# Softmax denominators of a memory attention: nine bf16 blocks on TensorE, or a GpSimd sum in three bf16 terms

## The chip, the cores and the metric

The kernel runs on one core of a Trainium2 chip. The metric is the device time of one launch in microseconds, the median of the runs shown. All times inside the kernel come from one profiled execution on the chip.

## The reference

The program has two parts. The first is an attention through 32 memory slots per head; the second is a channel mix of the RWKV kind on its output. Shapes: q, k, v are (8, 8, 576, 64) for batch, head, position and head width, phi is (8, 8, 576, 32), all in f32.

```
a    = exp(phi - max over positions); a = a / (sum over positions of a + 1e-9)
k_m  = sum over s of a[s, m] k[s, d];   v_m likewise with v
attn = softmax over m of (q k_m^T / 8);  x = attn v_m        (heads joined: 8 x 576 x 512)
x_prev = x shifted by one position
xk = mu_k x + (1 - mu_k) x_prev;   xr likewise with mu_r
out = sigmoid(xr w_r) * (relu(xk w_k)^2 w_v)
```

What the change touches is the sum over positions of exp(phi), one number for each head and slot. The kernel leaves out the maximum, which cancels in the quotient.

## The kernel before

The 576 positions of a batch are laid out as 64 rows of 9, so that one batch of phi fills 128 partitions (2 groups of 64 rows) by 4 heads by 9 positions by 32 slots. `exp_phi` (L225, word `exp`) takes a batch of phi on ScalarE and writes bf16 `em`, 128 x 9 x 4 x 32; there are two `em` tiles, for even and odd batches, and two buffers `ph` for raw phi. `ekv` (L237, word `kv`) multiplies `em` with k and v on TensorE in 72 small matmuls. `esum` (L247, word `z`) does the denominators: nine matmuls, one for each of the nine positions of a row, each with a 128 x 128 block of `em` as weights and a two-column tile of ones as moving data, accumulated in PSUM; VectorE takes the reciprocal `rz`. `norm_k` and `norm_v` (words `nk`, `nv`) scale by it, and the attention goes on: `tk` transposes the keys, `q0`, `q1` (or, for batches 6 and 7, `qx`, a transposing DMA on the SP queue) the queries, `s0`, `s1` are scores, `l0` to `l3` the second softmax's denominators, `r..z` and `w..` its weights, `x0`, `x1` the values, copied out by ScalarE, and `dd`, `k0d`, `k2d`, `r0d`, `r2d` the mix with the previous position on VectorE.

The channel mix runs over tokens: `c0:` to `c8:` are key products with relu on ScalarE (L524) and square on VectorE (L528), `g:` the gates of 128 tokens (L543 to L551), `o:` the value products, their product with the gate (L567) and the stores on the SP queue, from four `o` buffers. All PSUM tiles share eight banks under one name.

Nothing is scheduled automatically. `PLAN` is a list of words written out by hand, and every word emits its instructions in that place, for all engines; each engine then runs its own in that order and waits on the others by semaphores. A number before the colon is the batch; `p:` words are first loads. `load` of batch b issues the four loads of batch b + 2 (phi, k, v, q, in the order of `LOADS`) from GpSimd's queue, which issues in order. A phi load may start once the exp two batches earlier has read its `ph` buffer; the k, v and q loads likewise follow their earlier readers. With `SUMS` empty, no batch has the word `zr`, and `sum_rows` isn't called.

In the attention of the first two batches the mix is folded into the value products (`mk`, `mr`, L288 to L449), and the `idle` matmuls of `busy2` (L195) fill a place where TensorE waits.

Of the kernel before, what the change touches and what calls it, by code (L numbers as in the profile page):

```python
# [15 lines left out]


PLAN = [
    "p:q:0a p:k:0b 0:exp1 0:exp0 0:k0c 0:z 0:qh0 0:k1c 0:hn0 0:ht0 0:s0 p:q:0b 0:hn1 p:v:0a 0:qh1 0:l0 0:ht1 0:l1",
    "0:s1 0:mub p:v:0b 0:l2 p:wr:0-4 p:wk:0-4 0:h1z 0:v0c 0:h0z 0:nr0 0:v1c p:phi:1 0:h2z 0:l3 0:y1 0:y0 p:wk:4-8",  # L20
    "0:h3z 0:nr1 0:busy2 0:y2 0:y3 0:nk0 0:nk1 0:mr0 0:mr1 0:mk0 0:mk1 c0:2a c0:0a g:2 1:exp c0:3a c0:2b c0:5b c0:4b",
    "g:3 1:z c0:6a g:0 p:k:1 1:k 1:nk c0:6b p:q:1 c0:7b c0:0b c0:3b 1:q0 1:q1 0:mu 1:tk c0:5a c0:1a c0:4a p:v:1 1:s1",
    "1:s0 c0:1b 1:v 1:l2 1:l0 c0:7a 1:nr0 p:wv:0-2 p:wv:2-4 1:nk0 1:h0z 1:l3 1:l1 1:h2z 1:nr1 1:h1z 1:h3z g:1 o:3a",
    "1:y2 1:y3 o:2a 1:nk1 1:y0 1:y1 o:2b o:3b 1:mk1 o:0a 1:mk0 1:mr0 c1:0 c1:2 c1:4 1:mr1 g:4 c1:6 c1:3 0:load 2:exp",
    "g:5 2:q0 2:q1 o:1a 7:load 2:z 2:kv 2:nk 2:nv o:0b 2:tk c1:1 2:s1 2:s0 c1:7 c1:5 2:l0 2:l2 2:l1 2:l3 2:r0z 2:r1z",
    "2:w0 2:w1 o:1b o:5 o:4 1:load 3:exp 2:x0 3:q0 g:6 3:z 3:q1 3:kv 2:x1 3:nk g:7 3:nv 3:tk 2:dd 2:k0d g:8 3:s0 3:s1",
    "2:load 2:k2d o:6 4:exp o:7 2:r0d 3:l0 c2:1 c2:5 3:l3 3:l2 4:z 3:l1 c2:0 3:r1z 3:w1 3:r0z 3:w0 c2:4 2:r2d c2:2",
    "c2:3 c2:7 3:x1 4:kv 3:load c2:6 3:x0 4:nk 4:nv g:10 3:dd 3:k0d g:11 3:k2d g:9 5:exp 4:tk 4:q1 4:q0 o:9 o:10 c3:7",
    "c3:0 o:8 5:z 4:s0 5:kv 4:load 3:r0d 4:s1 5:q1 6:exp 5:q0 6:qx 5:nk c3:5 c3:4 4:l1 3:r2d 4:l2 c3:3 5:nv 4:l3 4:l0",
    "5:tk 4:r1z c3:6 g:12 c3:2 6:z 6:kv 6:nv 5:s0 4:r0z 5:load 5:s1 4:w1 4:w0 c3:1 g:13 6:nk o:11 g:14 6:tk 4:x0 o:13",  # L30
    "4:x1 g:15 4:dd o:12 5:l3 4:k0d 5:l0 5:l1 5:r0z o:14 5:l2 4:k2d g:16 7:exp 4:r0d 5:r1z o:15 c4:1 c4:3 7:z 7:kv",
    "6:s1 5:w0 5:w1 6:s0 c4:5 c4:0 5:x0 7:nv 4:r2d 7:nk c4:2 6:l1 c4:4 c4:6 6:l2 c4:7 7:qx 6:l3 5:x1 5:dd g:18 5:k2d",
    "g:19 7:tk 6:l0 g:17 o:18 5:k0d 6:r1z o:16 o:19 7:s1 6:r0z 7:s0 c5:3 c5:1 c5:7 6:w0 g:20 7:l2 c5:2 6:w1 7:l0 7:l1",
    "c5:6 7:l3 5:r2d c5:0 c5:5 c5:4 7:r1z 5:r0d 6:x1 o:17 6:x0 g:21 7:r0z 6:dd 6:k2d o:20 o:21 7:w1 g:22 6:k0d g:23",
    "7:w0 o:23 o:22 6:r2d c6:2 7:x1 c6:5 c6:1 6:r0d 7:x0 c6:4 g:24 7:dd c6:0 6:load c6:7 c6:3 c6:6 g:25 g:26 7:k0d",
    "7:r0d 7:k2d g:27 o:25 o:24 o:26 c8:0 c7:5 c8:6 7:r2d g:28 o:27 g:29 c7:6 c7:0 c7:4 c8:2 g:30 c7:1 c7:2 c7:7 c7:3",
    "g:31 c8:7 c8:4 o:29 c8:3 o:28 o:31 g:32 c8:5 o:30 c8:1 g:33 g:34 o:33 g:35 o:32 o:34 o:35",
]

LOADS = {None: ("phi", "k", "v", "q"), 2: ("phi", "k", "q", "v"), 3: ("phi", "k", "q", "v"), 4: ("phi", "k", "q", "v")}  # L40
PRE = "k:0a id:"
SUMS = ()


NJ = 9
# [4 lines left out]
def kernel(  # L50
# [13 lines left out]
    nc = tc.nc  # L64
# [146 lines left out]
    def attention(b):  # L211
        st = {}

        def ps_tile(shape, dtype, name):
            return psum.tile(shape, dtype, name=name, tag="ps", bufs=8)
# [5 lines left out]
        x0 = b * S % RING  # L221
        kv5, em = kvs[b % 2], ems[b % 2]
# [20 lines left out]
        def esum():  # L243
            st["zps"] = ps_tile([128, 2], F32, "zps")
            parts = [em[:, j].rearrange("p h m -> p (h m)") for j in range(NJ)] if b not in SUMS else st["es"]
            for i, part in enumerate(parts):
# [5 lines left out]
        def sum_rows():  # L252

            left = work.tile([128, HH * M], F32, name="es", tag="es", bufs=1)
            nc.vector.reduce_sum(left, em.rearrange("p j h m -> p (h m) j"), axis=mybir.AxisListType.X)
            terms = work.tile([128, 3, HH * M], BF16, name="et", tag="et", bufs=1)
            for i in range(3):
                nc.vector.tensor_copy(terms[:, i], left)
                if i < 2:
                    nc.vector.tensor_sub(left, left, terms[:, i])  # L260
            st["es"] = [terms[:, i] for i in range(3)]

        def hold():
# [173 lines left out]
        def mixed(w, hf):  # L437

            def go():
# [7 lines left out]
                for i in range(ND):  # L447
# [5 lines left out]
        steps = {"exp": exp_phi, "kv": ekv(slice(0, 2)), "k": ekv(slice(0, 1)), "v": ekv(slice(1, 2)),  # L453
                 "z": esum, "nk": norm_k(), "nv": norm_v, "tk": tr_k(), "load": reload, "mu": load_mu, "mub": load_mu_b, "qx": cross_q,
                 "zr": sum_rows, "hold": hold}
        for i in range(2):
            steps[f"q{i}"] = tr_q(i)
# [163 lines left out]
```

## Time and profile before

| | |
|---|---|
| median of 3 runs | 208.88 us (208.71 to 209.04) |
| profiled execution | 208.39 us, its span 206.6 us |
| mean granted TensorE clock | 0.999 |
| HBM read, written | 38.28 MB, 9.44 MB |
| exp(phi) of a whole batch, L225 | 7 times, 1166 ns |
| phi loads by GpSimd | 7, 576 KB each, median 15.7 us from issue to landing |
| key squares on VectorE, L528 | 104 instructions, 32.7 us |
| mixes on VectorE, L423 and L424 | 48 times 364 ns, 24 times about 759 ns |

In the span's rows PE is the matmul part of TensorE, PEld its weight loads, DVE is VectorE, ACT ScalarE, POOL GpSimd, SP the engine that issues stores. A group's line names engine, operation, what it writes and reads, the count, busy time and mean duration, and the idle time of the engine before it. A matmul's duration is its latency; matmuls follow one another at a shorter pitch. Idle time of an engine that isn't on the chain that ended last costs nothing. The time of the execution is 1.8 us longer than the span.

### The profile page before, as it was taken

The page shows a single profiled execution, that of the slowest core. Times are in us where ns is not written, and L with a number is a line of the kernel's source. Part 1 is how long each engine was busy: PE and PEld are TensorE (multiplying, and loading weights), DVE is VectorE, ACT ScalarE, POOL GpSimd, SP SyncE. Part 2 cuts the span into 40 slices and gives each one's busy share as a digit, 9 for nine tenths or more (in the row PEclk, how much of TensorE's full clock was granted, in tenths as well). Part 3 has the DMA queues.
Part 4 walks back from the last instruction along what each step waited for, and adds up shares of the span by engine and source line. Part 5 has one row for each costly group of instructions (what it writes and reads, how often), then busy time and mean ns, then how long its engine had stood idle before and what let it go on. Part 6 is the DMA issues. An engine that isn't in the chain of part 4 may idle for free.

```text
span 206.6 us, 5609 instructions
## 1 busy us (share of the span) xinstructions
PE 193.9 (94%) x2269; PEld 103.5 (50%) x2269; DVE 135.4 (66%) x364; ACT 159.5 (77%) x314; POOL 29.4 (14%) x45
## 2 busy tenths in 40 slices
PE   0499999999999999999999999999999999999992
PEld 0355676746555545466445764444434444444451
DVE  1129445866478989988749779487978944533232
ACT  3256899978778999978999799989878955882570
POOL 7652422201414102150000000000000000000000
PEclk9999999999999999999999999999999999999999
DMA  6999999999999999999999850502260062004335
GB/s 161 173 204 262 210 208 202 261 230 285 215 273 239 256 279 213 260 231 307 208 157 211 126 87 16 124 17 52 54 154 0 0 152 54 0 0 112 91 71 135
DMA packets 29274, 32.49 MB, mean 157 GB/s; under 512 B 6704, under 2 KB 24384, under 8 KB 29248
## 3 DMA queue, kind: packets, MB, share of 16 engines
q0 software_dynamic: 17392, 20.91, 53.8%
q1 hardware_dynamic: 11088, 10.37, 23.3%
q10 hardware_dynamic: 768, 0.85, 1.3%
q8 instruction: 18, 0.29, 0.6%
q14 instruction: 8, 0.07, 0.1%
HBM read 38.28 MB, written 9.44 MB: 231 GB/s over the span
## 4 chain that ended last, share of the span: by engine, by line
PE 92%; DMA 3%; POOL 1%; DVE 1%; issue 1%; POOLq 0%; DVEq 0%
PE pk L520 31%; PE pv L565 31%; PE pr L543 15%; PE kvps L237 4%; DMA kv<-in_k_dram 3%; PE mxps L288 2%; PE zps L372 2%; PE scps L358 2%; PE qtps L339 2%; PE nops L288 2%; PE zps L247 1%; PE ktps L301 1%; PE mub L200 1%; PE qtps L326 1%; DVE o L567 0%
## 5 line engine op out<-in xcount | busy, mean ns | idle before, releaser
L520 PE MATMUL pk<-xkT,wk 128*128 128x512 bf16 (+4 forms) x352 | 69.0, 341 | 0.0
L565 PE MATMUL pv<-wv,sq 128*128 128x512 bf16 (+1 forms) x328 | 66.2, 353 | 0.0
L528 DVE TENSOR_TENSOR sq<-rl 128x512 bf16<-128x512 bf16 (+5 forms) x104 | 32.7, 341 | 33.3 <-ACT rl L524 32.5
L524 ACT ACTIVATE rl<-pk 128x512 bf16<-128x512 f32 (+3 forms) x80 | 42.9, 560 | 13.4 <-PE pk L520 10.6
L520 PEld LDWEIGHTS <-wk 128*128 128x128 bf16 x352 | 32.7, 98 | 27.8 <-issue 1.6
L565 PEld LDWEIGHTS <-sq 128*128 128x128 bf16 x328 | 31.5, 98 | 29.9 <-issue 0.5
L543 PE MATMUL pr<-wr,xrT 128*128 128x512 bf16 x144 | 35.8, 380 | 0.0
L567 DVE TENSOR_TENSOR o<-sg,pv 128x512 f32<-128x512 f32 (+1 forms) x41 | 24.9, 620 | 15.0 <-PE pv L565 8.7
L548 ACT ACTIVATE sg<-pr 128x512 f32<-128x512 f32 x36 | 21.5, 610 | 8.8 <-PE pr L543 8.8
L543 PEld LDWEIGHTS <-xrT 128*128 128x128 bf16 x144 | 13.5, 98 | 14.8 <-issue 0.2
L550 ACT ACTIVATE sg<-sg 128x1024 f32<-128x1024 f32 x18 | 19.0, 1057 | 0.6
L551 ACT ACTIVATE sg<-sg 128x1024 f32<-128x1024 f32 x18 | 19.0, 1057 | 0.6
L401 ACT CAST x<-nops 128x320 bf16<-128x320 f32 (+1 forms) x48 | 15.7, 419 | 2.4 <-PE nops L288 2.3
L237 PE MATMUL kvps<-kv,em 64*32 64x128 bf16 (+1 forms) x720 | 8.7, 218 | 7.8 <-DMA kv<-in_k_dram 7.8
L423 DVE TENSOR_SCALAR mu_d<-diff,mu 128x576 bf16<-128x576 bf16 x48 | 15.5, 364 | 0.1
L362 ACT ACTIVATE e<-scps 128x320 bf16<-128x320 f32 (+1 forms) x32 | 11.0, 415 | 4.3 <-PE scps L358 4.2
L389 DVE TENSOR_TENSOR atn<-e,lz 128x576 bf16<-128x576 bf16 (+2 forms) x20 | 12.0, 631 | 1.4 <-ACT lz L382 1.3
L377 ACT ACTIVATE lz<-zps 128x320 f32<-128x320 f32 (+1 forms) x32 | 11.7, 413 | 0.8 <-PE zps L372 0.8
L237 PEld LDWEIGHTS <-em 64*32 64x32 bf16 x720 | 7.5, 95 | 8.9 <-ACT em L225 6.1
L225 ACT ACTIVATE em<-ph 128x1152 bf16<-128x1152 f32 (+1 forms) x9 | 9.4, 1056 | 2.3 <-DMA ph<-in_phi_dram 2.3
L382 ACT ACTIVATE lz<-lz 128x576 f32<-128x576 f32 (+2 forms) x20 | 11.1, 587 | 0.1
L413 DVE TENSOR_TENSOR diff<-x 128x1024 bf16<-128x1024 bf16 (+1 forms) x18 | 9.0, 552 | 2.4 <-ACT x L401 2.4
(65 smaller groups left out, 143.7 us busy)
## 6 DMA issues: line engine op xcount, KB each, us to landing
out_dram<-o SPq DMA_DIRECT2D x61, 128.0 KB, 2.4
ph<-in_phi_dram POOLq DMA_DIRECT2D x7, 576.0 KB, 15.7
kv<-in_k_dram POOLq DMA_DIRECT2D x7, 576.0 KB, 15.8
q<-in_q_dram POOLq DMA_DIRECT2D x7, 576.0 KB, 17.9
kv<-in_v_dram POOLq DMA_DIRECT2D x7, 576.0 KB, 19.3
out_dram<-o SPq DMA_DIRECT2D x18, 64.0 KB, 5.5
wk<-in_moe_w_k_dram POOLq DMA_DIRECT2D x2, 512.0 KB, 14.8
wv<-in_moe_w_v_dram POOLq DMA_DIRECT2D x2, 512.0 KB, 20.3
```

The costliest lines, as they stand in the source:

```text
L237: nc.tensor.matmul(kvps[c][g * M:(g + 1) * M], lhsT=em[ROWS[c], j, g, :], rhs=kv5[ROWS[c], parts, g, j, :], start=j == 0, stop=j == NJ - 1 ...
L401: nc.scalar.copy(st["x"][:, i, sl], pss[i])
L423: nc.vector.tensor_scalar_mul(t[:, i], st["d"][:, pr + i, :], mu1[:, o:o + 1])
L520: nc.tensor.matmul(pk[:, p0 - lo:p1 - lo], lhsT=wk_sb[:, di, fi * 128:(fi + 1) * 128], rhs=xk_T[:, di, p0 % RING:p0 % RING + p1 - p0], sta ...
L524: nc.scalar.activation(rl, pk, AF.Relu)
L528: nc.vector.tensor_mul(sq[:, fi, p:p + p1 - p0], rl[:, p0 - lo:p1 - lo], rl[:, p0 - lo:p1 - lo])
L543: nc.tensor.matmul(pr, lhsT=xr_T[:, di, c0:c0 + 128], rhs=wr_sb[:, di, :], start=(di == 0), stop=(di == ND - 1))
L548: nc.scalar.activation(sg[:, t % 2], pr, AF.Exp, scale=-1.0)
L550: nc.scalar.activation(sg, sg, AF.Ln, bias=1.0)
L551: nc.scalar.activation(sg, sg, AF.Exp, scale=-1.0)
L565: nc.tensor.matmul(pv[:, cols], lhsT=sq[:, fi, p:p + 128], rhs=wv_sb[:, fi, cols], start=(fi == 0), stop=(fi == NF - 1))
L567: nc.vector.tensor_mul(o[:, cols], gated[t // 2][:, t % 2, cols], pv[:, cols])
```

## The change

For batches 2 to 7, `SUMS` is filled and the list has a word `zr`. `sum_rows` then has GpSimd add the nine 128 x 128 blocks of `em` into an f32 tile with eight adds, and split the sum into three bf16 terms: convert, subtract, convert, subtract, convert. `esum` takes these three terms as weights in place of the nine blocks, so that it has three matmuls instead of nine. The f32 tile and the terms have one buffer each. The whole list is in a new order; besides the six `zr` words, its words are the same but for `busy2`, which is now `busy3`, with three idle matmuls. Batches 0 and 1 keep nine matmuls. In the new list every `load` from `1:load` to `5:load` stands behind the `zr` of the batch before the one that it loads.

```diff
--- before.py
+++ after.py
@@ -16,30 +16,31 @@
 
 
 PLAN = [
-    "p:q:0a p:k:0b 0:exp1 0:exp0 0:k0c 0:z 0:qh0 0:k1c 0:hn0 0:ht0 0:s0 p:q:0b 0:hn1 p:v:0a 0:qh1 0:l0 0:ht1 0:l1",
-    "0:s1 0:mub p:v:0b 0:l2 p:wr:0-4 p:wk:0-4 0:h1z 0:v0c 0:h0z 0:nr0 0:v1c p:phi:1 0:h2z 0:l3 0:y1 0:y0 p:wk:4-8",
-    "0:h3z 0:nr1 0:busy2 0:y2 0:y3 0:nk0 0:nk1 0:mr0 0:mr1 0:mk0 0:mk1 c0:2a c0:0a g:2 1:exp c0:3a c0:2b c0:5b c0:4b",
-    "g:3 1:z c0:6a g:0 p:k:1 1:k 1:nk c0:6b p:q:1 c0:7b c0:0b c0:3b 1:q0 1:q1 0:mu 1:tk c0:5a c0:1a c0:4a p:v:1 1:s1",
-    "1:s0 c0:1b 1:v 1:l2 1:l0 c0:7a 1:nr0 p:wv:0-2 p:wv:2-4 1:nk0 1:h0z 1:l3 1:l1 1:h2z 1:nr1 1:h1z 1:h3z g:1 o:3a",
-    "1:y2 1:y3 o:2a 1:nk1 1:y0 1:y1 o:2b o:3b 1:mk1 o:0a 1:mk0 1:mr0 c1:0 c1:2 c1:4 1:mr1 g:4 c1:6 c1:3 0:load 2:exp",
-    "g:5 2:q0 2:q1 o:1a 7:load 2:z 2:kv 2:nk 2:nv o:0b 2:tk c1:1 2:s1 2:s0 c1:7 c1:5 2:l0 2:l2 2:l1 2:l3 2:r0z 2:r1z",
-    "2:w0 2:w1 o:1b o:5 o:4 1:load 3:exp 2:x0 3:q0 g:6 3:z 3:q1 3:kv 2:x1 3:nk g:7 3:nv 3:tk 2:dd 2:k0d g:8 3:s0 3:s1",
-    "2:load 2:k2d o:6 4:exp o:7 2:r0d 3:l0 c2:1 c2:5 3:l3 3:l2 4:z 3:l1 c2:0 3:r1z 3:w1 3:r0z 3:w0 c2:4 2:r2d c2:2",
-    "c2:3 c2:7 3:x1 4:kv 3:load c2:6 3:x0 4:nk 4:nv g:10 3:dd 3:k0d g:11 3:k2d g:9 5:exp 4:tk 4:q1 4:q0 o:9 o:10 c3:7",
-    "c3:0 o:8 5:z 4:s0 5:kv 4:load 3:r0d 4:s1 5:q1 6:exp 5:q0 6:qx 5:nk c3:5 c3:4 4:l1 3:r2d 4:l2 c3:3 5:nv 4:l3 4:l0",
-    "5:tk 4:r1z c3:6 g:12 c3:2 6:z 6:kv 6:nv 5:s0 4:r0z 5:load 5:s1 4:w1 4:w0 c3:1 g:13 6:nk o:11 g:14 6:tk 4:x0 o:13",
-    "4:x1 g:15 4:dd o:12 5:l3 4:k0d 5:l0 5:l1 5:r0z o:14 5:l2 4:k2d g:16 7:exp 4:r0d 5:r1z o:15 c4:1 c4:3 7:z 7:kv",
-    "6:s1 5:w0 5:w1 6:s0 c4:5 c4:0 5:x0 7:nv 4:r2d 7:nk c4:2 6:l1 c4:4 c4:6 6:l2 c4:7 7:qx 6:l3 5:x1 5:dd g:18 5:k2d",
-    "g:19 7:tk 6:l0 g:17 o:18 5:k0d 6:r1z o:16 o:19 7:s1 6:r0z 7:s0 c5:3 c5:1 c5:7 6:w0 g:20 7:l2 c5:2 6:w1 7:l0 7:l1",
...
+    "0:exp1 0:exp0 7:load p:q:0a 0:z 0:mu 0:k0c 0:qh0 p:k:0b 0:hn0 0:ht0 0:k1c 0:hn1 0:s0 p:q:0b 0:qh1 0:ht1 p:v:0a",
+    "0:mub 0:l1 0:s1 0:h1z 0:v0c 0:l0 0:l2 p:v:0b 0:h0z 0:l3 0:h2z 0:v1c 0:nr0 p:wk:4-8 0:nk0 p:wr:0-4 0:y1 0:nr1",
+    "0:nk1 0:h3z 0:y0 p:phi:1 0:y2 0:y3 0:busy3 p:wk:0-4 0:mk0 0:mr0 c0:6a 0:mr1 0:mk1 1:exp c0:5a g:2 g:3 c0:1b",
+    "c0:5b c0:0a 1:z c0:0b p:k:1 g:0 c0:7a 1:k 1:nk c0:2b p:q:1 c0:3b c0:3a c0:7b 1:q0 1:q1 p:v:1 1:tk p:wv:0-2 c0:4a",
+    "c0:6b 1:s0 c0:1a 1:s1 1:v 1:l0 p:wv:2-4 1:l1 c0:2a 1:h1z 1:l3 c0:4b 1:l2 1:h3z 1:h2z 1:y1 1:y3 1:nk1 1:h0z 1:nr1",
+    "1:nk0 g:1 0:load 1:y2 1:nr0 o:2a 1:y0 o:3a o:2b o:1a 1:mk0 o:1b 1:mk1 o:3b 2:exp 2:zr 1:mr0 c1:0 1:mr1 c1:5 c1:6",
+    "g:4 c1:3 c1:2 g:5 2:z 2:q1 2:q0 o:0a 1:load 2:kv 2:nk o:0b 3:exp 2:tk 2:nv c1:7 2:s0 2:s1 3:zr c1:1 c1:4 2:l0",
+    "2:l2 2:l1 2:load 2:l3 2:r0z 2:r1z 2:w0 2:w1 g:6 g:7 o:5 3:q1 3:q0 o:4 3:z 2:x1 3:kv 3:nk 3:nv 2:x0 3:tk g:8 3:s1",
+    "2:dd 2:k0d 2:k2d 3:s0 4:exp o:6 3:l3 3:l1 3:l0 3:l2 o:7 3:r1z 3:r0z 4:zr 3:w0 c2:5 3:w1 c2:3 c2:0 2:r2d c2:6",
+    "c2:7 4:z 2:r0d 3:x0 c2:2 c2:1 c2:4 3:x1 3:load 3:dd 4:kv 4:nv 4:nk g:10 5:exp 3:k0d g:11 3:k2d 5:zr g:9 o:11",
+    "4:tk 4:q0 4:q1 o:10 c3:7 c3:3 4:load c3:0 5:z 5:kv 3:r2d 4:s1 6:qx 4:s0 5:nk c3:6 5:nv 3:r0d 4:l2 6:exp c3:4",
+    "c3:1 4:l3 5:tk c3:5 4:l1 g:12 c3:2 4:l0 5:q0 5:q1 6:zr 4:r0z g:13 o:8 6:z 4:w0 4:r1z 4:w1 6:kv 5:s0 5:s1 5:load",
+    "6:nv 6:nk 7:exp o:12 o:13 4:x1 g:14 4:x0 5:l0 4:dd 7:zr o:9 4:k0d 5:l1 4:k2d 5:r0z 5:w0 5:l3 g:15 o:14 g:16 5:l2",
+    "o:15 6:tk 5:r1z c4:5 c4:7 7:z 7:kv 4:r2d 6:s0 6:s1 5:w1 c4:3 c4:2 c4:4 5:x0 7:nk 7:nv 6:load c4:1 c4:6 c4:0 5:x1",
+    "7:tk 4:r0d 7:qx 5:dd 6:l3 g:17 6:l1 6:l2 5:k2d 5:k0d 5:r0d o:17 g:18 o:16 g:19 6:l0 o:18 5:r2d c5:2 6:r1z c5:6",
...
 ]
 
 LOADS = {None: ("phi", "k", "v", "q"), 2: ("phi", "k", "q", "v"), 3: ("phi", "k", "q", "v"), 4: ("phi", "k", "q", "v")}
 PRE = "k:0a id:"
-SUMS = ()
+SUMS = (2, 3, 4, 5, 6, 7)
 
 
 NJ = 9
@@ -252,12 +253,15 @@
         def sum_rows():
 
             left = work.tile([128, HH * M], F32, name="es", tag="es", bufs=1)
-            nc.vector.reduce_sum(left, em.rearrange("p j h m -> p (h m) j"), axis=mybir.AxisListType.X)
+            cols = em.rearrange("p j h m -> p j (h m)")
+            nc.gpsimd.tensor_add(left, cols[:, 0], cols[:, 1])
+            for j in range(2, NJ):
+                nc.gpsimd.tensor_add(left, left, cols[:, j])
             terms = work.tile([128, 3, HH * M], BF16, name="et", tag="et", bufs=1)
             for i in range(3):
-                nc.vector.tensor_copy(terms[:, i], left)
+                nc.gpsimd.tensor_copy(terms[:, i], left)
                 if i < 2:
-                    nc.vector.tensor_sub(left, left, terms[:, i])
+                    nc.gpsimd.tensor_sub(left, left, terms[:, i])
             st["es"] = [terms[:, i] for i in range(3)]
 
         def hold():
```

## The prediction

> **What bounds the kernel now.** I read the page first: span, busy shares, the chain that ended last.
>
> ```profile
> span 206.6 us, 5609 instructions
> PE 193.9 (94%) x2269; PEld 103.5 (50%) x2269; DVE 135.4 (66%) x364; ACT 159.5 (77%) x314; POOL 29.4 (14%) x45
> PE 92%; DMA 3%; POOL 1%; DVE 1%; issue 1%; POOLq 0%; DVEq 0%
> ```
>
> TensorE carries 92% of the chain. PE time taken out is therefore gained, and a wait put in front of PE is lost. The next view is busy time per 10 us over the stretch in which batches 2 to 7 enter.
>
> ```profile
> 42.00:52.00 10.00, 9.95 (x211) 5.50 (x196) 6.71 (x19) 8.31 (x16) 0.76 (x1) 1.00 1.17 258
> 62.00:72.00 10.00, 10.00 (x166) 5.21 (x165) 9.08 (x25) 8.80 (x20) 2.51 (x4) 1.00 1.18 243
> 82.00:92.00 10.00, 10.00 (x198) 5.62 (x190) 9.24 (x25) 8.42 (x13) 2.57 (x4) 1.00 1.18 241
> 102.00:112.00 10.00, 10.00 (x63) 4.58 (x62) 6.93 (x15) 9.67 (x21) 0.00 (x0) 1.00 1.26 151
> ```
>
> Columns: stretch, length, then PE, PEld, DVE, ACT, POOL busy, clock, DMA share, GB/s. PE is full at full clock. DVE (over 90% around 62 to 72 and 82 to 92) and ACT (97% at the end) have little to spare. POOL is nearly free, but it issues the loads; its timeline and, under it, the DMA view say how:
>
> ```profile
> 30.54 0.76 POOL L103 DMA_DIRECT2D ph<-in_phi_dram  x1 [2.09 <-ACT rl L524]
> 50.51 0.76 POOL L103 DMA_DIRECT2D ph<-in_phi_dram  x1 [11.02 <-ACT em L225]
> 60.44 0.76 POOL L103 DMA_DIRECT2D ph<-in_phi_dram  x1 [5.93 <-ACT em L225]
> ```
>
> ```profile
> ph<-in_phi_dram ACTq DMA_DIRECT2D x1, 576.0 KB, 4.0
> ```
>
> The first column is the start; brackets give POOL's idle time before and what ended it. Phi of batch 3 is issued at 30.54, 18 us before exp(phi) of batch 2 runs (49.06). Today a phi load waits for the exp two batches earlier, whose buffer it takes. Issue plus landing, stretch by stretch, puts phi of batches 2 to 7 in SBUF at 39.7, 52.2, 62.9, 76.2, 87.4 and 99.6: one per 12.0 us, the pace of a DMA system busy in tenths of 9 until 105 us. The last line is the one phi load that met empty queues: 4.0 us.
>
> **What goes.** Six batches lose six denominator matmuls each, L247:
>
> ```profile
> L247 PEld LDWEIGHTS <-em x72: 95/96/118, 7.7 to 114.6; 128*128 128x128 bf16 x72
> L247 PE MATMUL zps<-ones,em x72: 163/163/187, 7.7 to 114.6; 128*128 128x2 bf16 x72
> ```
>
> 163 ns is latency, not price. Nine of them take 0.37 us from first start to last end, so one costs (0.37 - 0.163)/8 = 26 ns, and 36 give **-0.93 us**. The page's chain agrees: L247 has 1% (0.7% in the finer answer, 1.45 us for 72, 20 ns each).
>
> **What is added: 13 POOL instructions a batch**, eight adds, three conversions and two subtractions of 128x128. The trace has no POOL add. The nearest row is the mask:
>
> ```profile
> masks.py:199 POOL TENSOR_SCALAR_AFFINE_SELECT identity<-identity 128x128 bf16<-128x128 bf16 x1 | 0.3, 289 | 0.1
> ```
>
> Low end: 13 x 0.289 = 3.8 us a batch. High end: each also waits for one mean DVE instruction (135.4/364 = 0.37): 13 x 0.66 = 8.6 us. Here a rule speaks against the change. The row first: POOL's phi issues take 756 to 767 ns whether DVE is at 28% or at 90%, so this trace shows no hindrance between them; but those issues read no tensor. The Trainium skill, "SBUF — State Buffer", section "Who interferes with whom", says that a VectorE instruction with two SBUF inputs, or in a two-port mode, and a GpSimd instruction reading SBUF exclude each other for a whole instruction. By the row alone a batch costs 3.8 us and DVE nothing. By the rule it costs up to 8.6, and DVE is held too. Of 55.2 us DVE work between 42 and 112 us, the lines with two SBUF inputs or a scaled bf16 copy (L528 10.4, L423 6.4, L424 7.4, L389 4.4, L413 4.5) are 33 us, 47% of the 70 us. I take the middle, **6.2 us a batch**.
>
> **Where it lies.** I added each word's PE pitch along both lists (keys and gates 0.865 us, values 1.73, mixes 0.87, kv 0.67, scores 0.2, from runs in the chain) from the first mix at 17.95. For the old list this gives the z words of batches 2 to 7 at 51.2, 62.2, 71.4, 88.1, 95.8, 112.8; the trace has 50.8, 62.4, 71.9, 89.3, 97.1, 114.4. So the tally is good to 2 us. The new list:
>
> - exp words: 42.7, 53.6, 65.4, 78.2, 88.8, 97.9
> - z words: 50.5, 62.9, 73.7, 86.7, 96.8, 111.9
>
> The sum has some 8 us between exp and z, 14 in batch 7. It needs exp 1.17 + 6.2 = 7.4. That alone just fits. But **POOL is in order, and every load is now behind a sum**: the load of batch 3 stands behind zr of batch 2, batch 4 behind zr of 3, and so on to 7 behind 6. There is a new loop: exp, sum, phi issue and landing, next exp, of 1.17 + 6.2 + 4.0 = 11.4 us on empty queues. That is just under the 12.0 us at which DMA delivers, so DMA still sets the pace, but its lead is gone.
>
> Start: exp of batch 2 at about 43.3; sum done 50.7; phi of batch 3 lands at 54.7 (52.2 before). With 12.0 per batch: 66.7, 78.7, 90.7, 102.7. Against the exp words ScalarE is late by 1.1, 1.3, 0.5, 1.9 and 4.8 us. Sums are ready 7.4 later: 62.1, 74.1, 86.1, 98.1, 110.1. Against the z words: on time, +0.4, on time, +1.3, on time. These lags don't add, since the largest shifts all that follows: **+1.3 us** of PE.
>
> **ScalarE.** It too is in order: exp of batch 7 stands at 97.9 + 1.3 = 99.2 and phi comes at 102.7, so it holds 3.5 us. Behind it are the x copies of batch 4, a gate, the logarithms. PE has o:12 and o:13 (3.5 us) before it needs PSUM back, so it doesn't wait at once; but ACT from 92 to 112 is busy 18.75 of 20 us, and only 1.25 can be made up: **+2.2 us**. Bounds 0 and 3.5. The same stretch holds a second lag. 6:qx, a transposing load on SP, waits for q of batch 6 (10.6 us after phi before, so 101.3) and takes 6.4; output stores behind it start at 107.7, and o:14 needs a buffer one of them frees. It falls in the same hold, so I add nothing, up to 2 us more if it outlasts it. The early loads end with v: batch 3's v lands 9.2 us after phi (61.4 against 52.2), at 63.9 for a kv at 63.2; inside the 1.3.
>
> **DVE.** If each of 78 POOL instructions held DVE for half its own time (0.145), that is 11.3 us in all, 4.8 of them in the 30 us from 62 to 92, where DVE has 30 - 27.0 = 3.0 to spare: 1.8 lost by the rule, nothing by the row. I take **+0.9**.
>
> **Start and end.** Tiles, loads and order of the first loads stay; the first half's transpose comes before the second half's keys, the mu product before the second scores, and a third idle matmul (0.43) is added where PE waits 0.84 for DVE anyway. From -0.6 (first scores need not queue behind keys landing at 10.37) to +0.6 (second scores behind the 1.2 us mu product): 0. At the end both lists close on gate 35 and value 35: 0. The other moved words cost PE the same; the old order has 3.8 us of small waits up to its last matmul (tally 198.8, trace 202.6), and the new one may have 2 fewer or more.
>
> **Sum.** -0.9 + 1.3 + 2.2 + 0.9 = +3.5 us. The profiled execution took 208.39 (206.6 span and 1.8 around it), giving 211.9; the median shown is 0.49 higher, so **212.4 us**.
>
> **Rivals.**
> A, *the sums fit* (chance 0.28): at the mask's 3.8 us the loop is 9.0 us against 12.0; sums are ready 5.0 us after phi, before every z word; phi comes 2.4 us earlier than in my times, so ACT's hold at exp of batch 7 shrinks to about 2.4 us, less than the 3.5 us of value products that PE has ahead of it; DVE isn't held. Then -0.9, 208.0, and down to 206.2 if the new order also sheds half of the old 3.8 us of small waits. For it: the row, and POOL's empty second half. Against: DVE's 90%.
> B, *the loop sets the pace* (0.12): at 8.6 us the loop is 13.8. Five rounds fall 9 us behind 12.0, and 5 x 2.4 = 12 us behind my times; batch 6's sum comes at 98.1 + 4 x 2.4 + 2.4 = 110.1 against 96.8, PE loses 13: 220 us. It decides from a sum of 6.8 us on, where the loop passes 12.0. For it: two-input DVE work throughout. Against: POOL would have to wait at every instruction.
> C, *no change* (0.06): gains and waits cancel, 208.4 to 209.3.
> My forecast, 209.3 to 217, has 0.54.
>
> The slower side is my forecast's 0.54 and B's 0.12: 0.66; faster is A's 0.28, within 0.2% C's 0.06. What a measurement can tell from no change is about 0.2%, 0.4 us. The range takes most of A, C and my own: 206.8 to 217; outside are most of B and the edge of A.
>
> **What would show it.** Sums of about 6 us on POOL; phi of batch 3 issued near 51, not 30.5; ACT waits of several us at exp of batch 7 on the phi DMA; small PE waits before L247 in batches 4 and 6; longer DVE instructions at L424 and L528 in that stretch. It would be wrong if POOL's instructions are near 0.29 us with none between them, if phi lands before its exp all the same, or if the new order removes waits that I take as fixed.

## The result and the profile after

The changed kernel takes 224.18 us (median of 4 runs, 222.62 to 226.75) against 208.96 us before: a ratio of 1.069, 95% interval 1.062 to 1.077. The profiled execution took 223.67 us, 221.9 of them span. The forecast side was right; the size, 3.5 us, was less than a quarter of the 15.2 us measured, and the time lies outside the range. Ratios, here and below, leave out runs over 1.5% above the fastest of the same kernel (one of these four, eight of nineteen with loads ahead and sums unused, five of six in the last experiment), so a ratio may differ a little from that of two medians.

The page of the kernel after, in the same parts as before (span, busy time, the chain by engine):

```profile
span 221.9 us, 5600 instructions
PE 197.2 (89%) x2212; PEld 104.2 (47%) x2234; DVE 139.9 (63%) x364; ACT 160.3 (72%) x314; POOL 66.9 (30%) x123
PE 55%; DMA 20%; POOL 12%; issue 4%; ACT 4%; DVE 2%; SPq 0%; POOLq 0%; DVEq 0%; ACTq 0%
```

PE held 92% of the chain; now DMA and POOL have 32% of it. GpSimd's busy time rose from 29.4 to 66.9 us. That alone costs nothing; that it entered the chain is the finding. The chain is one path of several: by line the queries' loads have 7% of it and phi's only 2%, so what each is worth is left to the experiments. The same four stretches as before:

```profile
42.00:52.00 10.00, 9.47 (x135) 5.02 (x135) 6.41 (x17) 7.94 (x15) 6.79 (x15) 1.00 0.88 183
62.00:72.00 10.00, 8.78 (x173) 4.75 (x176) 8.22 (x22) 8.73 (x21) 5.25 (x9) 1.00 1.07 219
82.00:92.00 10.00, 9.89 (x155) 5.05 (x156) 8.86 (x24) 9.41 (x16) 5.30 (x11) 1.00 1.15 224
102.00:112.00 10.00, 8.22 (x152) 4.18 (x151) 6.40 (x17) 7.09 (x14) 7.64 (x15) 1.00 0.87 174
```

PE was 9.95 to 10.00 of 10 us in all four; now it has holes, and the DMA share before the last column is down from 1.17 to 0.88 in the first stretch: DMA, too, has pauses. The timeline of POOL shows one sum and the load behind it (start, duration, engine; in brackets the idle time before):

```profile
86.52 0.42 POOL L257 TENSOR_TENSOR es<-em 128x128 f32<-128x128 bf16 x1 [4.01 <-ACT em L226]
87.02 4.39 POOL L259 TENSOR_TENSOR es<-es,em 128x128 f32<-128x128 f32 x7
91.48 0.29 POOL L262 CAST et<-es 128x128 bf16<-128x128 f32 x1
...
94.10 0.79 POOL L104 DMA_DIRECT2D ph<-in_phi_dram  x1 [0.61 <-issue]
```

and the same view of ScalarE shows what comes before and after it, exp of batches 2 to 7:

```profile
43.05 1.18 ACT L226 ACTIVATE em<-ph 128x1152 bf16<-128x1152 f32 x1
55.29 1.16 ACT L226 ACTIVATE em<-ph 128x1152 bf16<-128x1152 f32 x1 [2.01 <-DMA ph<-in_phi_dram]
70.03 1.20 ACT L226 ACTIVATE em<-ph 128x1152 bf16<-128x1152 f32 x1
85.22 1.15 ACT L226 ACTIVATE em<-ph 128x1152 bf16<-128x1152 f32 x1
99.44 1.16 ACT L226 ACTIVATE em<-ph 128x1152 bf16<-128x1152 f32 x1 [2.50 <-DMA ph<-in_phi_dram]
112.14 1.16 ACT L226 ACTIVATE em<-ph 128x1152 bf16<-128x1152 f32 x1 [2.26 <-DMA ph<-in_phi_dram]
```

Follow one round. Exp of batch 5 starts at 85.22; the sum starts at 86.52 and ends at 93.5; phi of batch 6 is issued at 94.10 and lands 5.0 us later; exp of batch 6 starts at 99.44, having waited 2.50 us for that DMA. From batch 2 on the five rounds take (112.14 - 43.05)/5 = 13.8 us each. Before, they took (111.62 - 49.06)/5 = 12.5, but with the words in other places; the new list without its sums takes 11.9 (an experiment below). Three of the five rounds end in a wait for phi. In the other two, to batches 4 and 5, phi had landed 1.2 us before its exp: ScalarE came to it late, behind work that on the chain follows the queries of batch 3, loaded behind a sum too, and the sum of batch 4.

A second hole comes at the end of that stretch. SP's transposing load for batch 6 (the word 6:qx) began at 108.16, once q of batch 6 had landed (108.02), and held SP for 10.8 us. Output stores stood behind it; VectorE needed an output buffer, with the key copy of batch 6 behind that on its queue. VectorE, then PE, then the clock in 2 us stretches:

```profile
126.82 1.28 DVE L571 TENSOR_TENSOR o<-sg,pv 128x512 f32<-128x512 f32 x2 [4.32 <-DMA out_dram<-o]
```

```profile
128.36 0.73 PE L362 MATMUL scps<-qT,kmT 64*32 64x320 bf16 x16 [4.05 <-DVE kmT L309]
```

```profile
126.00:128.00 2.00, 0.00 (x0) 0.00 (x0) 1.18 (x2) 0.00 (x0) 0.00 (x0) 0.57 1.05 395
128.00:130.00 2.00, 1.64 (x22) 0.98 (x23) 1.97 (x10) 1.11 (x4) 0.00 (x0) 0.50 0.62 147
130.00:132.00 2.00, 2.00 (x11) 1.39 (x10) 1.62 (x4) 0.81 (x2) 0.00 (x0) 0.50 0.56 127
132.00:134.00 2.00, 2.00 (x19) 1.25 (x17) 0.56 (x3) 0.71 (x2) 0.00 (x0) 0.72 0.71 116
```

The third column from the right is the granted clock. PE waits 4.05 us, the clock falls to half, and the matmuls up to about 133 us are slow: 24 key products take 4.78 us there, and the next 24, from 134 us on, 2.79. So some 2 us of PE time are lost beside the 4.05.

### The profile page after: what moved, and what is told of

Same layout as the page of the kernel before. It is cut to its first block, busy times and chain, and to the rows that moved or that the text cites. A ratio compares the mean times of both kernels' runs of the same rounds, so it can differ in the third digit from the quotient of the medians.

```text
span 221.9 us, 5600 instructions
## 1 busy us (share of the span) xinstructions
PE 197.2 (89%) x2212; PEld 104.2 (47%) x2234; DVE 139.9 (63%) x364; ACT 160.3 (72%) x314; POOL 66.9 (30%) x123
## 4 chain that ended last, share of the span: by engine, by line
PE 55%; DMA 20%; POOL 12%; issue 4%; ACT 4%; DVE 2%; SPq 0%; POOLq 0%; DVEq 0%; ACTq 0%
PE pv L569 20%; PE pk L524 20%; PE pr L547 9%; DMA q<-in_q_dram 7%; DMA wk<-in_moe_w_k_dram 7%; POOL es L259 7%; DMA out_dram<-o 3%; DMA ph<-in_phi_dram 2%; ACT em L226 2%; POOL et L262 2%; PE kvps L238 2%; POOL es L264 2%; PE nops L292 1%; ACT x L405 1%; DVE o L571 1%
## 5 line engine op out<-in xcount | busy, mean ns | idle before, releaser
L524 PE MATMUL pk<-xkT,wk 128*128 128x512 bf16 (+4 forms) x344 | 69.9, 349 | 1.1 <-DMA wk<-in_moe_w_k_dram 0.7
L532 DVE TENSOR_TENSOR sq<-rl 128x512 bf16<-128x512 bf16 (+5 forms) x104 | 33.8, 351 | 29.6 <-ACT rl L528 28.8
L524 PEld LDWEIGHTS <-wk 128*128 128x128 bf16 x352 | 34.0, 101 | 30.5 <-issue 1.8
L547 PE MATMUL pr<-wr,xrT 128*128 128x512 bf16 x138 | 35.2, 379 | 0.3
L552 ACT ACTIVATE sg<-pr 128x512 f32<-128x512 f32 x36 | 21.3, 605 | 10.8 <-DVE o L571 5.3
L259 POOL TENSOR_TENSOR es<-es,em 128x128 f32<-128x128 f32 x42 | 22.2, 529 | 3.3
L405 ACT CAST x<-nops 128x256 bf16<-128x256 f32 (+1 forms) x48 | 15.6, 419 | 4.1 <-PE nops L292 4.1
L427 DVE TENSOR_SCALAR mu_d<-diff,mu 128x576 bf16<-128x576 bf16 x48 | 16.8, 392 | 0.1
L393 DVE TENSOR_TENSOR atn<-e,lz 128x576 bf16<-128x576 bf16 (+2 forms) x20 | 12.5, 650 | 1.3 <-ACT lz L386 1.3
L381 ACT ACTIVATE lz<-zps 128x256 f32<-128x256 f32 (+1 forms) x32 | 12.4, 444 | 1.2 <-PE zps L376 1.1
L257 POOL TENSOR_TENSOR es<-em 128x128 f32<-128x128 bf16 x6 | 2.7, 443 | 33.3 <-ACT em L226 33.3
L386 ACT ACTIVATE lz<-lz 128x576 f32<-128x576 f32 (+2 forms) x20 | 11.3, 600 | 0.2
## 6 DMA issues: line engine op xcount, KB each, us to landing
q<-in_q_dram POOLq DMA_DIRECT2D x7, 576.0 KB, 11.7
wk<-in_moe_w_k_dram POOLq DMA_DIRECT2D x2, 512.0 KB, 13.9
```

Of the source, the lines that this page charges most:

```text
L259: nc.gpsimd.tensor_add(left, left, cols[:, j])
L405: nc.scalar.copy(st["x"][:, i, sl], pss[i])
L427: nc.vector.tensor_scalar_mul(t[:, i], st["d"][:, pr + i, :], mu1[:, o:o + 1])
L524: nc.tensor.matmul(pk[:, p0 - lo:p1 - lo], lhsT=wk_sb[:, di, fi * 128:(fi + 1) * 128], rhs=xk_T[:, di, p0 % RING:p0 % RING + p1 - p0], sta ...
L532: nc.vector.tensor_mul(sq[:, fi, p:p + p1 - p0], rl[:, p0 - lo:p1 - lo], rl[:, p0 - lo:p1 - lo])
L547: nc.tensor.matmul(pr, lhsT=xr_T[:, di, c0:c0 + 128], rhs=wr_sb[:, di, :], start=(di == 0), stop=(di == ND - 1))
```

## The experiments

**Theory 1**: loads wait behind sums, and a loop of exp, sum and phi load sets the pace. **Theory 2**: TensorE waits for the sums in front of L248. **Theory 3**: the new order is slow by itself. The first four runs part them.

**Loads ahead of the sums.** The loads of batches 3 to 7 go in front of the sum that they stood behind. For batches 6 and 7 only phi, k and v go (`lp`); q keeps its place (`lq`), since its readers come later in the list.

```diff
-2:exp 2:zr ... o:0a 1:load 2:kv
+2:exp 1:load 2:zr ... o:0a 2:kv
-2:s1 3:zr ... 2:l1 2:load 2:l3
+2:s1 2:load 3:zr ... 2:l1 2:l3
-3:r0z 4:zr ... 3:x1 3:load 3:dd
+3:r0z 3:load 4:zr ... 3:x1 3:dd
-3:k2d 5:zr ... c3:3 4:load c3:0
+3:k2d 4:lp 5:zr ... c3:3 4:lq c3:0
-5:q1 6:zr ... 5:s1 5:load
+5:q1 5:lp 6:zr ... 5:s1 5:lq
```

> All sums stay and L248 still takes the three terms; only the loads are moved ahead of the sums on GpSimd (the q loads of batches 6 and 7 stay where they were). Theory 1, loads wait behind sums: phi of batch 3 is issued near 31 us again, exp goes back to a round of about 12 us, the time falls to 209 to 213 us. Theory 2, TensorE waits for the sums themselves in front of L248: each sum still takes about 7 us, so the time stays at 220 us or more. Theory 3, the new order of the list is slow by itself: above 218 us.

Measured: 212.24 us (211.98 to 212.97), ratio to before 1.015 (1.010 to 1.020). From 224.18 that is 11.9 us back with every sum still there. ScalarE's and POOL's timelines of this run, for exp of batches 2 and 7 and phi of batch 3:

```profile
43.40 1.18 ACT L228 ACTIVATE em<-ph 128x1152 bf16<-128x1152 f32 x1
...
105.83 1.19 ACT L228 ACTIVATE em<-ph 128x1152 bf16<-128x1152 f32 x1
```

```profile
31.34 0.75 POOL L104 DMA_DIRECT2D ph<-in_phi_dram  x1 [2.09 <-ACT rl L530]
```

Phi of batch 3 is issued at 31.34 instead of 50.87, no exp of batches 2 to 7 waits for DMA, and a round takes (105.83 - 43.40)/5 = 12.5 us, 1.3 less than in the kernel after. Theory 1.

**The new order without sums.** `SUMS = ()` and no `zr` words.

> The new list without its six sum words, and nine blocks on TensorE as before. Theories 1 and 2: the time is that of the kernel before within 1% (207 to 211 us). Theory 3, the new order is slow by itself: 215 us or more.

Measured: 209.27 us, ratio 1.0001 (0.998 to 1.003). Theory 3 falls: the new order, the mu product's new place and the third idle matmul are together worth nothing either way. This is also the list to compare rounds with; exp of batches 2 and 7:

```profile
42.73 1.18 ACT L226 ACTIVATE em<-ph 128x1152 bf16<-128x1152 f32 x1
...
102.05 1.18 ACT L226 ACTIVATE em<-ph 128x1152 bf16<-128x1152 f32 x1
```

A round takes (102.05 - 42.73)/5 = 11.9 us, and no exp of batches 2 to 7 waits for a load. The sums add 1.9 us to the mean round in the kernel after, and 0.6 with the loads ahead.

**Sums run, but unused.** The complement of the first run:

```diff
-parts = [... for j in range(NJ)] if b not in SUMS else st["es"]
+parts = [... for j in range(NJ)]
```

> The sums run on GpSimd in their places, but TensorE takes the nine blocks and never waits for them. Theory 1, loads wait behind sums: nothing is gained, 221 to 227 us. Theory 2, TensorE waits for the sums: 208 to 213 us.

Measured: 222.15 us, ratio 1.061 (1.054 to 1.068). TensorE has no wait for a sum any more (4.4 us in the kernel after), and only some 2 us come back, which the intervals of the two ratios don't tell from nothing. Its waits, longest in total (us, times, longest):

```profile
PE zps L248 <- ACT em L226: 5.9, 1, 5.9
PE scps L362 <- DMA out_dram<-o: 2.9, 1, 2.9
PE zps L376 <- ACT rl L528: 2.1, 1, 2.1
```

The first is the start, where the first z word now stands in front of the first keys; it is in the run without sums as well. The second is the hold of the stores, the third ScalarE stuck in front of a late phi. Theory 2 by itself is at most a side effect.

**The transposing load later.** `6:qx` goes from its place before `4:s0` to behind `o:9`, so that four tiles' stores pass ahead of it.

> The kernel after, with the transposing load of batch 6's queries moved behind four output tiles (o:8, o:12, o:13, o:9) on the SP queue. If the stores held behind it cost the 4.1 us wait of PE at 124 us and the half clock after it, the time falls by 4 to 7 us, to 217 to 220 us. If the late queries of batch 6 hold PE instead, it stays at 222 us or more.

Measured: 222.02 us, ratio 1.059 (1.052 to 1.067), 2.2 us less, under the 4 expected, and the intervals of the two ratios overlap; the time just meets the second answer. The wait moves rather than goes:

```profile
PE scps L362 <- DMA qT<-q: 2.3, 2, 1.5
```

PE now waits for the queries themselves, which are late because their load is. With the loads ahead, TensorE has no wait at these scores in the trace, so the stores' hold is mostly a consequence of the late loads.

The second four ask how long a sum is, and what is left once the loads are early.

**A shorter sum.** The blocks are added 512 wide, then folded:

```diff
-nc.gpsimd.tensor_add(left, cols[:, 0], cols[:, 1])
-for j in range(2, NJ):
-    nc.gpsimd.tensor_add(left, left, cols[:, j])
+nc.gpsimd.tensor_add(wide, flat[:, 0:512], flat[:, 512:1024])
+nc.gpsimd.tensor_add(wide[:, 0:256], wide[:, 0:256], wide[:, 256:512])
+nc.gpsimd.tensor_add(left, left, wide[:, 128:256])
+nc.gpsimd.tensor_add(left, left, flat[:, 1024:1152])
```

> The kernel after, with the nine blocks added in four instructions (512, 256, 128 and 128 wide; the same 1024 sums of elements, in the space of mu_m, which is free by then) instead of eight. Where the loop of exp, sum, phi load sets the pace, every us by which a sum is shorter comes back five times: with 0.5 to 1.2 us less, the time falls by 2.5 to 6 us, to 218 to 222 us. If only a fixed place in the order matters and not the length, it stays at 223 us or more.

Measured: 218.99 us, ratio 1.046 (1.042 to 1.051). From start of the first add to end of the last conversion the six sums take 5.7, 6.2, 6.8, 5.9, 5.3 and 5.8 us, mean 5.9, where the kernel after has 6.6, 7.4, 8.2, 7.0, 6.7 and 7.1, mean 7.15. So each is 1.2 us shorter, five rounds take 65.5 us instead of 69.1, and the time falls by 5.2 us. The rounds account for 3.6 of them. In this trace TensorE also waits for no sum any more, so the run doesn't separate the loop from that wait. One instruction of each width:

```profile
110.08 1.15 POOL L257 TENSOR_TENSOR mu_m<-em 128x512 f32<-128x512 bf16 x1 [4.17 <-ACT em L226]
111.30 0.73 POOL L258 TENSOR_TENSOR mu_m<-mu_m 128x256 f32<-128x256 f32 x1
...
112.64 0.42 POOL L261 TENSOR_TENSOR mu_m<-mu_m,em 128x128 f32<-128x128 f32 x1
```

From 128 to 512 elements 0.42 goes to 1.15 us: 1.9 ns an element, and about 0.18 us that each instruction has whatever its width. Four instructions fewer save that and the gaps between them.

**Loads ahead, sums unused.**

> Loads ahead of the sums, sums run on GpSimd, but TensorE takes nine blocks and doesn't wait for them. The 3 us that e1 is still above e2: if TensorE's wait for the sums makes them (each sum has about 8 us between exp and its z word and takes about 7), they go, and the time is 209 to 210 us. If VectorE, held at its SBUF port by GpSimd's instructions, makes them, it stays at 211 to 213 us.

Measured: 211.55 us (209.40 to 217.14) over nineteen runs. The eleven from 209.40 to 212.08, whose median is 210.8, give the ratio of 1.007 (1.004 to 1.010), between the two answers. Against 1.015 with the sums used and 1.000 without sums, about half of what was left, 0.8%, goes with TensorE's wait for the sums, and 0.7% stays although nobody waits for them. VectorE's busy time, 135.2 us without sums, is 139.8 in the run with loads ahead, so the port is a candidate for that half; it wasn't parted from other effects of a busy GpSimd. The intervals of this run and of the first just touch, so the halves are rough. The trace of this run is of one of the other eight executions (214.09 us). In it the stores' hold is back although the loads are early: VectorE stands 3.29 us for a store, PE 2.26 us in front of the scores of batch 6, and half clock follows. So early loads alone don't rule that hold out.

**Loads ahead and the shorter sum.**

> Loads ahead and the sum in four wide instructions. If what is left in e1 is TensorE's wait for the sums, a shorter sum takes part of it: 209.5 to 211.5 us. If it is the port, the wide adds hold VectorE for longer at a time and nothing is gained: 212 us or more.

Measured: 211.45 us, ratio 1.012 (1.006 to 1.017): within the intervals of the run with loads ahead, so no gain can be told. TensorE waits for no sum in this trace and VectorE is busy for 141.9 us, so the run doesn't confirm that half of the rest was the wait for the sums. No version with the sums beat the kernel before.

**Loads ahead and the transposing load later.**

> Loads ahead, and the transposing load of batch 6's queries behind four output tiles on the SP queue. If stores held behind it cost anything once the loads are early, the time falls below e1's 212.2 us by 1 us or more; if the hold only followed from the late loads, it is e1's within 0.5%.

Measured: 214.48 us, ratio 1.025 (1.021 to 1.030), 2.2 us slower than loads ahead alone, which neither answer foresaw. With early loads the queries are in time, and moving their transposes back makes them late: PE waits 1.4 us for them at the scores.

The last two ask which of the loads matters, and what the clock costs.

**Only phi ahead.** The edit of the first run for phi alone; k, v and q stay behind the sums.

> Only phi of the five loads is moved ahead of the sums; k, v and q of batches 3 to 7 stay behind them. Theory 1a, late phi makes the loop (exp waits for phi, the next sum for exp): the rounds of exp fall from 13.8 to about 12.5 us, and the time goes most of the way to e1's 212.2 us: 211 to 216 us. Theory 1b, late k, v and q hold TensorE at kv and the queries, phi was only the first of them: 218 us or more.

Measured: 216.19 us, ratio 1.035 (1.031 to 1.038), just above the band of 1a. Rounds of exp are 12.7 us ((106.09 - 42.63)/5), so the loop is all but gone (exp of batch 7 waits 0.25 us for phi), and 8.0 of the 11.9 us with it. The other 4 belong to k, v and q: TensorE still stands at the scores of batch 6 for stores held by late queries, and waits for sums:

```profile
PE zps L250 <- POOL et L264: 3.6, 7, 1.1
PE scps L364 <- DMA out_dram<-o: 1.9, 1, 1.9
```

**Idle matmuls in the wait.** `0:busy16` in front of `6:s0`.

> The kernel after, with 16 idle matmuls (about 3.5 us at full clock) in front of the scores of batch 6, where TensorE waited 4.05 us and its clock then was at half for some 5 us. If the clock fell because TensorE stood idle, and its half speed costs, the stretch after the wait runs at full clock and the time falls by 1.5 to 2.5 us. If the clock fell for another reason, or the slow matmuls were hidden, it stays within 0.5% of 224.2 us. If idle matmuls only lengthen the wait, it rises by up to 3 us.

Measured: 228.05 us (222.78 to 229.52). Five of the six runs took 226.66 us or more, at a mean clock of 0.970 to 0.985; the sixth took 222.78 at 1.000, no longer than the kernel after. In the trace, of an execution of 226.66 us, the filling matmuls had to wait 2.52 us themselves, until VectorE had read a product from PSUM, and started at 128.33. About 1.1 us later the clock fell all the same, so that they took 5.30 us in PE's timeline:

```profile
128.33 5.30 PE L196 MATMUL idle<-zeros 128*128 128x512 bf16 x16 [2.52 <-DVE o L571]
```

This trace also has half clock from 109.0 to 112.1 us, which the kernel after doesn't, and the five longer runs rise by up to 5.3 us where the third answer allows 3. So none of the three answers is shown, and what the half clock costs by itself stays open.

## Why the prediction was wrong in size

**What was right.** The new loop was named, with its members and order, and "every load is now behind a sum" is what the runs show. Two of the named signs came: phi of batch 3 was issued at 50.87, and PE waited in front of the z words of batches 4 and 6, up to 1.09 us at a time. The zero for start and end, and for the moved words, holds to 0.3% (the run without sums). 212.4 us is what the kernel takes with its loads ahead, which is chance: there the loop that I counted on is gone.

**The step that failed** is "That is just under the 12.0 us at which DMA delivers, so DMA still sets the pace". It rested on two terms and a pace. The sum, put at 6.2 us, measured 7.15. Its low end came from a 289 ns mask row, and an add takes longer even with nothing in its way:

```profile
L259 POOL TENSOR_TENSOR es<-es,em x42: 427/431/826, 44.8 to 117.3; 128x128 f32<-128x128 f32 x42
```

Minimum, median and maximum: 427 ns at the least, and a pitch of 0.50 us. Eight adds of 0.50, two subtractions of 0.49 and three conversions of 0.37 make 6.1 us unhindered. My middle value was thus the true low end, and holds by VectorE came on top (below). Phi's landing, put at the 4.0 us of the first load, measured 4.4 to 5.0. With 1.2 for exp and about 0.5 of gaps the loop is 1.2 + 7.15 + 4.7 + 0.5 = 13.5 us. From the start of one exp to the landing of the next phi the trace has 12.2, 13.5, 13.9, 13.9 and 12.6 us, each above 12.0.

The pace of 12.0 us was not DMA's either. Before the change phi of batches 3 to 7 landed 3.9 to 12.1 us ahead of its exp, no exp of batches 2 to 7 waited for a load, and three of the phi issues waited for an exp. The loads followed the list; a loop of 11.4 us had no slower DMA to hide behind.

So rival B happened in the main. It gave a point of decision, 6.8 us, which 7.15 passes; a loop of 13.8 us, from a longer sum (8.6) and a shorter landing than were measured; and 220 us. That its 13.8 equals the mean round is chance, as two rounds did not end at phi. Its sum has a slip: my times already advance by 12.0 a batch, so a loop of 13.8 falls behind by 1.8 a round, not 2.4, and the sum of batch 6 comes at 108.3, not 110.1 (measured: 107.4). Nor did PE lose its time in front of the sums alone: 4.4 us there, 4.05 in front of the scores of batch 6, some 2 to the clock, and the rest in smaller pieces. B had a chance of 0.12 because I set its point of decision against a sum of 8.6 rather than asking how near 6.2 was to 6.8. "These lags don't add, since the largest shifts all that follows" fails with it: once a loop sets the pace, a lag can add in every round. With each sum shorter by 1.2 us the five rounds fell by 3.6 us.

**The SP queue.** "It falls in the same hold, so I add nothing, up to 2 us more" was too little. The queries landed at 108.0, not 101.3, the transposes took 10.8 us, not 6.4, and VectorE stood for 4.32 us. Why the transposes took longer isn't shown: loads of batch 7 were in flight beside them before the change as well. The fall of the clock behind it was not in the sum at all.

**DVE.** I put 11.3 us of hold on VectorE and lost 0.9 of them. Its busy time grew by 4.5 us. The rule that I weighed (the Trainium skill, "SBUF — State Buffer", section "Who interferes with whom": the two exclude each other for a whole instruction) is borne out by this trace, and the row of phi issues was no evidence against it. Of the 60 adds and subtractions 38 took 420 to 431 ns. The other 22, of 486 to 826 ns, had all begun beside a VectorE instruction with two inputs in SBUF or, twice, a scaled bf16 copy of L427, and each ended 0.28 to 0.29 us after that instruction's end. VectorE is held in turn: its mixes, which hardly left 759 ns without sums, reach 923 here. One such pair, and the mixes:

```profile
87.78 0.92 DVE L428 TENSOR_TENSOR xkT<-x,mu_d 128x1152 bf16<-128x1152 bf16 x1
88.17 0.83 POOL L259 TENSOR_TENSOR es<-es,em 128x128 f32<-128x128 f32 x1
```

```profile
L428 DVE TENSOR_TENSOR xkT<-x,mu_d x12: 757/759/923, 70.6 to 184.7; 128x1152 bf16<-128x1152 bf16 x12
```

**The gain.** The -0.93 us for 36 matmuls can't be seen in any run by itself, next to the much larger costs.

## What to carry to other kernels

An engine that is nearly free in busy time may still own an in-order queue that others need: before work is put on it, list what is issued behind that work, and check whether the chain through it closes into a loop that repeats in every round. If it does, compare the loop's length with the round's, not with the idle time, and treat the estimate as a threshold: a term as near to its deciding value as 6.2 is to 6.8 deserves nearly even chances. Where a queue must carry both, issue the loads first.

## What the runs showed of the hardware

- A GpSimd add of f32 took 0.42, 0.73 and 1.15 us at 128, 256 and 512 elements a partition. By these rows some 0.26 of the 0.50 us from one narrow add to the next has nothing to do with its elements (an estimate).
- TensorE's wait of 4.05 us began at 124.3; its clock fell to 0.50 at about 126.2 and stayed there for 6.9 us. Waits of 1.91 us (only phi ahead), 2.26 us (loads ahead, sums unused) and 2.80 us (shorter sum) had the same fall at their end or shortly before or after, for 3.4 us; one of 1.51 us (transposing load later) did not. In the last experiment's trace it fell at 109.0 us after two waits of 0.68 us. The Trainium skill, "TensorE: Matmul & The Clock Gate", section "Part 1: The HAM clock gate", puts the fall after at least one idle window of about 3.4 us; here less idle time was enough, and no limit can be read from these traces.
- Phi landed 4.4 to 5.0 us after its issue when it was held back, against 11.7 to 21.7 us before the change, when it ran ahead. The shorter latency belongs to the slower kernel: a load that lands late after its issue but long before its use costs nothing.
